# Shift parts given out one at a time in the front, and branch A's sums of group 0 on GpSimd

## The chip, the cores and the metric

The kernel runs on one core of a Trainium2 chip. The time is the device time of one execution in microseconds (us), the median of the runs. Engines are named as in the profile: PE (TensorE matmul), PEld (its weight loads), DVE (VectorE), ACT (ScalarE), POOL (GpSimd), SP (SyncE, which here only issues DMAs). "SPq" is SP's queue. L12 is line 12 of the kernel before.

## The reference

Two attention branches on the same x (1 x 2048 x 512, float32) are mixed by a gate per position:

```
g = sigmoid(sum(x * gate_w))                       # per position
a = A(x):  q, k, v = x @ A_wqkv  (32 heads of 16)
           each position attends to itself and to 7 earlier ones, 2 apart (mask below 0)
           out = softmax(q.k * 16**-0.5) . v, then @ A_wo
b = B(x):  q = x @ B_wq (32 heads of 16), ONE k = x @ B_wk and v = x @ B_wv for all heads
           full softmax over 2048 keys, then @ B_wo
out = g * a + (1 - g) * b
```

## The kernel before

**The stages.** The kernel has a front and a second phase. In the front, PE computes branch B's keys and queries, and then branch A's projections. In the second phase 512 steps compute branch B's softmax: for each unit (one of 32: four blocks of 512 queries by eight head groups) and each of 16 key tiles PE makes scores (L460), ACT takes exponentials (L462), and PE adds up the weighted values (L470). Branch A's local attention runs on POOL meanwhile (`a_load`, `a_scores`, `a_values`), and at four places PE projects the outputs (`out_phase`, L731).

**The maxima.** B's softmax needs each row's maximum before the exponentials: for each unit 64 products of 128 queries by 512 keys must be made on PE and reduced on DVE. They are "fills", put between PE's other work wherever the planner finds room: pairs in bank `pm` (`fill_pair`, L350) and singles in `ps` or `po` (`fill_one`, L361). In most of branch A's projections another form is used, of which one fill stands for four maxima: PE makes half the difference of two products (`fill_diff`, L409), ACT takes its absolute value (L418), PE makes half their sum (`fill_sum`, L409), and DVE adds and reduces (L428).

**The shifts.** When all 64 maxima of a unit are there (`filled`), DVE reduces and transposes them (L340, L342), ACT rounds them (`shift_a`, L434), POOL makes the remainder `ml` (`shift_c`, L440 and L441), and eight DMAs of 2 KB write the pieces into two extra rows of the unit's query tile `qst` (`shift_b`, L449). The scores then come out with the maximum subtracted. While branch A has work left (`pieces`), all eight are issued from SP. Query tiles exist for eight units, so the front can hold the maxima of eight units (512 of the 2048 products) at most.

**Branch A's projections.** They are 64 "lumps": 4 groups of heads (gg) by 16 position tiles (j). Each lump is 24 matmuls on half the rows (L956), the lower rows to one half of a PSUM bank and the upper rows to the other, and the two halves have to be added. Banks `eb[0]` and `eb[1]` alternate. For group 0 a lump is 402 columns wide instead of 384: it also holds B's v and the gate's sum. There the kernel before copies one half to `two` on ACT (L241), and DVE adds the other from PSUM in three additions (L246 to L249, into `stage`, `vst` and `gate`). For groups 1 to 3 (`a_add`) ACT copies both halves, one straight into the stage buffer (L265, L266), and POOL adds (L272). Every second lump one store writes the stage buffer to the scratch tensor `ad` in memory: in group 0 from ACT's queue (L253), in groups 1 to 3 from SP's (L276). There are two stage buffers, so a buffer is used again after four lumps. After the last lump of a group, `whole` makes its heads available to `a_load`; after group 0 it also starts the gate (`gates`, L283 to L291).

**The order.** The schedule is written out by the program itself, with a planner's clock: `clk` holds an assumed time for PE, ACT and DVE, `pool` one for POOL (in ns), and `free` says when a bank is free. All these are constants of the program, not measurements. A task list holds tuples of a due time and a function; `run_tasks`, called after every third matmul step, emits what is due by PE's clock, in the order of the list. `settle(kind, n)` emits all tasks of a kind but the last n at once. `run_pool` gives out branch A's pieces while `pool` is less than 2500 ns ahead of PE's clock. Each engine executes its instructions in the order in which they were emitted, and so does each DMA queue: a DMA that waits for its data holds up the ones behind it. In `stream`, which puts the projections and the fills together, a new pair of differences is emitted when the last fill's sums are out and

```
max(free["m2"], clk["dve"] - 0.7) <= clk["pe"] + 0.1
```

Of the kernel before, what the change touches and what calls it, by code (L numbers as in the profile page):

```python
# [6 lines left out]
F32 = mybir.dt.float32  # L7
F32R = mybir.dt.float32r
AF = mybir.ActivationFunctionType
# [4 lines left out]
P = 128  # L14
# [3 lines left out]
DH = 16  # L18
NJ = S // P
# [7 lines left out]
HALO = (W - 1) * DIL  # L27
# [5 lines left out]
AN = 3 * AC  # L33
GC = P // AC
GN = GC * AN
VN = DH + 2
NB = 8
# [7 lines left out]
T_R, T_LAT, T_EXP, T_RED2, T_RED1, T_W, T_TTR = 0.23, 0.20, 0.92, 1.14, 0.61, 1.21, 0.66  # L45
# [3 lines left out]
def gated_mix_kernel(ctx, tc, xt, wa, wk, wq, wo_a, wo_b, out):  # L49
# [30 lines left out]
    def after(eng, ready, dur):  # L80
        clk[eng] = max(clk[eng], ready) + dur
        return clk[eng]
# [142 lines left out]

    def a_post(gg, j, x):

        (bank, key), n = front[x], GN + (0 if gg else VN)
        for kind in ("post0", "post1", "add") if not gg else ("post0", "post1"):
            settle(kind, 0)  # L230
        if j % 2 == 0:
            settle("store", 1)
            stage["t"] = p1.tile([P, GC, 2, AN], F32, name="stage", bufs=2)
        st = stage["t"]
        if gg:
            return a_add(gg, j, x, st, bank, key)
        if j < 3:
            two = wp.tile([P, GN + VN], F32, name="two", tag="aext", bufs=2)
        else:
            two = pm[0].tile([P, GN + VN], F32, name="two", bufs=1)  # L240
        nc.scalar.activation(two[:, :n], bank[:, 1, :n], AF.Copy)  # L241
        at = after("act", clk["pe"] + T_LAT, 0.45) + 0.1
        free[key] = at + 1.5

        def rest():
            nc.vector.tensor_add(st[:, :, j % 2, :], bank[:, 0, :GN].rearrange("p (g n) -> p g n", g=GC), two[:, :GN].rearrange("p (g n) -> p g n", g=GC))  # L246
            if gg == 0:
                nc.vector.tensor_add(vst[:, j, 0:DH], bank[:, 0, GN:GN + DH], two[:, GN:GN + DH])
                nc.vector.tensor_add(gate[:, 1, j:j + 1], bank[:, 0, GN + DH:GN + DH + 1], two[:, GN + DH:GN + DH + 1])  # L249
            free[key] = after("dve", at, 0.5 if gg else 0.75) + 0.1  # L250
            if j % 2 == 1:
                dst = ad[gg * GC:(gg + 1) * GC, HALO:, :].rearrange("g (p j) n -> p g (j n)", j=NJ)
                tasks.append((free[key], lambda: nc.scalar.dma_start(dst[:, :, (j - 1) * AN:(j + 1) * AN], st.rearrange("p g j n -> p g (j n)")), (), "store"))  # L253
            if j == NJ - 1:
                tasks.append((free[key] + 0.5, whole, (gg,)))

        tasks.append((at, rest, (), f"post{x % 2}"))

    def a_add(gg, j, x, st, bank, key):

        settle("add", 1)
        tag = ("two", "raw", "own")[j % 3]
        two = (p2 if j % 3 else pm)[0].tile([P, GN], F32, name="two", tag=tag, bufs=1)
        own = st[:, :, j % 2, :]
        nc.scalar.activation(own, bank[:, 0, :GN].rearrange("p (g n) -> p g n", g=GC), AF.Copy)  # L265
        nc.scalar.activation(two, bank[:, 1, :GN], AF.Copy)  # L266
        at = after("act", clk["pe"] + T_LAT, 0.8)
        free[key] = at + 0.1

        def rest():  # L270
            nonlocal pool
            nc.gpsimd.tensor_add(own, own, two.rearrange("p (g n) -> p g n", g=GC))  # L272
            pool = max(pool, 1e3 * at) + 1000
            if j % 2 == 1:
                dst = ad[gg * GC:(gg + 1) * GC, HALO:, :].rearrange("g (p j) n -> p g (j n)", j=NJ)
                tasks.append((pool / 1e3 + 0.5, lambda: nc.sync.dma_start(dst[:, :, (j - 1) * AN:(j + 1) * AN], st.rearrange("p g j n -> p g (j n)")), (), "store"))  # L276
            if j == NJ - 1:
                tasks.append((pool / 1e3 + 1.0, whole, (gg,)))

        tasks.append((at, rest, (), "add"))  # L280
# [162 lines left out]
        shift_b(v, ml)  # L443

    def shift_b(v, ml):
        for b in range(2):
            dst = qst[v % NB][64 * b + 62:64 * b + 64].rearrange("x i (t q) -> x i t q", t=4).bitcast(F32)
            for g in range(4):
                (nc.gpsimd if b and not pieces else nc.sync).dma_start(dst[:, :, :, 32 * g:32 * g + 32], ml[32 * g + 16 * b:32 * g + 16 * b + 16, :].bitcast(F32))  # L449
        shifted.add(v)  # L450


    pe, pexp, exped = [], {}, {}
# [228 lines left out]
    def stream(seq, mm, done, pooled):  # L682

        at, told = [0, 0], 0
        ended.clear()
        while min(at) < len(seq):
            single, odd = None, -1
            if pend:
                if free[("m1", "po")[pend[0][4]]] <= clk["pe"] + 0.1 and ready_d[pend[0][4]] <= clk["pe"] + 0.4:
                    single, odd = fill_sum, pend[0][4]  # L690
            elif paired() and not half:
                pass
            elif fillable() and free["m1"] <= clk["pe"] + 0.1:
                single, odd = lambda: fill_one(m1, "m1"), half[0][4] if half else 0
            elif pooled and fillable() and free["po"] <= clk["pe"] + 0.1:
                single, odd = lambda: fill_one(po, "po"), half[0][4] if half else 0
            dur = 0.0
            for b in (0, 1) if odd != 1 else (1, 0):
                if b == odd:
                    now = clk["pe"]  # L700
                    single()
                    clk["pe"] = now
                elif at[b] < len(seq):
                    dur = mm(b, seq[at[b]])
                    at[b] += 1
            after("pe", 0, dur or T_R)
            if ended:
                pass
            elif paired():
                if not half and not pend and max(free["m2"], clk["dve"] - 0.7) <= clk["pe"] + 0.1:  # L710
                    fill_diff()
            elif slots and fillable() and free["m2"] <= clk["pe"] + 0.1:
                clk["pe"] = max(clk["pe"], free["m2"])
                fill_pair(m2, "m2")
            while told < min(at):
                told += 1
                done(seq[told - 1])
# [81 lines left out]
    def settle(kind, n):  # L799
        for task in [t for t in tasks if t[3:] == (kind,)][:-n or None]:  # L800
            tasks.remove(task)
            task[1](*task[2])
# [133 lines left out]
    def mm(b, at):  # L936
        nonlocal pool
        x, i = at
        lump = lumps[x]
        if x not in items:  # L940
            if lump[0] == "a" and lump[1:] == (0, 0):
                settle("rest", 0)
                p0.release()
                branch_a()
                pm.append(tc.alloc_tile_pool(name="maxima", bufs=1, side="right"))
            settle(f"post{x % 2}", 0)
            if lump == ("a", 0, 3):
                half_sel()
            elif lump in (("a", 0, 4), ("a", 0, 6)):
                half_keys(1 if lump[2] == 4 else 0)  # L950
            items[x] = queries(lump[1]) if lump[0] == "q" else a_project(*lump[1:])
            clk["pe"] = max(clk["pe"], free["m2" if x == last else f"e{x % 2}"])
        n = 512 if lump[0] == "q" else GN + (0 if lump[1] else VN)
        l, r = items[x][i]
        h = slice(64 * b, 64 * b + 64)
        nc.tensor.matmul(front[2 if x == last else x % 2][0][:, b, :n], l[h], r[h], start=(i == 0), stop=(i == 3 * C - 1))  # L956
        return T_R if n == 512 else 0.18

    def done_mm(at):
        nonlocal pool  # L960
        x, i = at
        lump = lumps[x]
        if i % 3 == 2:
            run_tasks()
            if p2:
                run_pool()
        if x == last - 1 and i == 3 * C - 2:
            ended.add(1)
        if x == last and i in (2, 7):
            settle(f"post{(i - 1) % 2}", 0)  # L970
            exp_pair(0, int(i == 2))
        if i < 3 * C - 1:
            return
        if lump[0] == "q":
            m = lump[1]
            queries_post(m, eb[x % 2])
            free[f"e{x % 2}"] = clk["act"]
            ahead_wa(0, m - 4)
        else:
            gg, j = lump[1:]  # L980
            a_post(gg, j, 2 if x == last else x % 2)
            if gg + 1 < C:
                ahead_wa(gg + 1, j - 2)
# [8 lines left out]
    stream([(x, i) for x in range(len(lumps)) for i in range(3 * C)], mm, done_mm, True)  # L992
    assert not pend
    formed.clear()
    for kind in ("post0", "post1", "add", "store"):
        settle(kind, 0)
    while [t for t in tasks if len(t) > 3]:
        clk["pe"] += 0.2
# [109 lines left out]
```

## Time and profile before

| what | value |
|---|---|
| time, median of 3 runs | 1537.48 us (1534.87 to 1542.45) |
| profiled execution | 1539.43 us, span 1537.6 us from the first to the last instruction |
| mean granted clock of PE | 0.992 |
| busy share PE / DVE / ACT / POOL | 97% / 81% / 80% / 66% |
| group 0, first L241 to last store's issue | 84.3 to 132.4 us |
| groups 1 to 3, first L265 to last L265 | 134.7 to 293.4 us |
| last maxima (L330) | before 1470 us |

PE's busy time is that of pipelined matmuls, so 97% is not 97% of what PE could do. A share over the span says little here, because the stages have different limits; the prediction goes by the stage that the change touches. "Granted clock" is the share of full speed at which the chip lets PE run.

### The profile page before, as it was taken

How to read it: one execution, taken by the hardware profiler on the slowest of the kernel's cores; microseconds unless marked ns; L12 is line 12 of the kernel's file. 1: busy time of each engine (PE TensorE's matmuls, PEld its weight loads, DVE VectorE, ACT ScalarE, POOL GpSimd, SP SyncE). 2: the span in 40 equal slices, each digit the busy share in tenths (PEclk: the TensorE clock that was granted, in tenths of full speed). 3: DMA queues.
4: the chain of work that ended last, by engine and by line, in shares of the span. 5: the costliest groups of instructions: out<-in, count | busy, mean ns of one | idle time of the engine just before them, and what ended most of it. 6: DMA issues, size and time to landing. Idle time of an engine off the chain costs nothing.

```text
span 1537.6 us, 29033 instructions
## 1 busy us (share of the span) xinstructions
PE 1491.8 (97%) x11020; PEld 717.7 (47%) x11020; DVE 1250.2 (81%) x1794; ACT 1232.9 (80%) x1532; POOL 1016.9 (66%) x1725
## 2 busy tenths in 40 slices
PE   7999988999999999999999999999999999999997
PEld 4989878633333333333333453333453354333532
DVE  6987555688888889888898998888998899888821
ACT  4547766888999999999999759999759966998676
POOL 7833867888978888888988988888886132000320
PEclk9999989999999999999999999999999999999999
DMA  6743223220120211211211112202110000000000
GB/s 214 203 116 130 74 73 94 79 75 22 65 70 16 85 51 43 68 46 40 75 40 41 67 39 68 62 18 68 41 57 22 2 15 16 2 2 1 2 1 28
DMA packets 43908, 85.63 MB, mean 56 GB/s; under 512 B 9520, under 2 KB 25960, under 8 KB 39672
## 3 DMA queue, kind: packets, MB, share of 16 engines
q1 hardware_dynamic: 31976, 40.85, 8.9%
q0 software_dynamic: 6560, 37.95, 7.3%
q10 hardware_dynamic: 5232, 4.98, 1.0%
q8 instruction: 86, 1.41, 0.4%
q14 instruction: 54, 0.44, 0.1%
HBM read 57.97 MB, written 25.25 MB: 54 GB/s over the span
## 4 chain that ended last, share of the span: by engine, by line
PE 85%; DVE 5%; ACT 4%; POOL 2%; SPq 1%; DMA 1%; issue 1%; DVEq 0%; ACTq 0%; POOLq 0%
PE po L470 32%; PE pe L460 22%; PE pm L330 9%; PE ps L330 8%; PE pe L956 5%; PE pe L731 5%; ACT pexp L462 3%; DVE mx L350 3%; DVE mx L361 2%; SPq L449 1%; PE pe L174 1%; PE pm L409 1%; POOL stage L272 1%; DMA ad<-stage 1%; ACT dd L418 1%
## 5 line engine op out<-in xcount | busy, mean ns | idle before, releaser
L462 ACT ACTIVATE pexp<-pe 128x1024 f32<-128x1024 f32 x1024 | 991.7, 1022 | 98.8 <-PE pe L460 95.9
L350 DVE TENSOR_REDUCE mx<-pm 128x2 f32<-128x1024 f32 x563 | 687.1, 1220 | 125.1 <-PE pm L330 120.2
L470 PE MATMUL po<-pexp,vst 128*32 128x512 f32 x4096 | 545.5, 605 | 1.0 <-DVE tt L484 0.5
L460 PE MATMUL pe<-qst,kst 64*128 64x512 f32 x2048 | 464.8, 450 | 9.8 <-ACT pexp L462 4.8
L460 PEld LDWEIGHTS pe<-qst,kst 64*128 64x128 f32 x2048 | 191.3, 183 | 514.1 <-ACT pexp L462 500.5
L361 DVE TENSOR_REDUCE mx<-ps 128x1 f32<-128x512 f32 x568 | 385.8, 679 | 5.5 <-PE ps L330 4.7
L330 PE MATMUL pm<-kst,qst 62*128 62x512 f32 x1139 | 239.7, 408 | 2.3 <-DVE mx L350 1.8
L330 PE MATMUL ps<-kst,qst 62*128 62x512 f32 x568 | 230.6, 406 | 0.8 <-DVE mx L361 0.8
L530 POOL TENSOR_TENSOR pr<-aext 128x256 f32<-128x256 f32 x256 | 182.6, 741 | 2.6 <-DMA aext<-ad 2.4
L590 POOL TENSOR_TENSOR oa<-oa,av 128x256 f32<-128x256 f32 x224 | 164.3, 733 | 15.1
L470 PEld LDWEIGHTS po<-pexp,vst 128*32 128x32 f32 x4096 | 80.5, 108 | 179.4 <-issue 166.4
L587 POOL TENSOR_TENSOR av<-aext,lg 128x256 f32<-128x256 f32 x224 | 139.6, 623 | 13.5
L496 POOL TENSOR_TENSOR rl<-rl,gate_t 128x16 f32<-128x16 f32 x31 | 6.9, 222 | 180.5 <-DVE rl L490 180.3
L330 PEld LDWEIGHTS pm<-kst,qst 62*128 62x128 f32 x1139 | 110.4, 186 | 27.2 <-DVE mx L350 23.1
L330 PEld LDWEIGHTS ps<-kst,qst 62*128 62x128 f32 x568 | 105.7, 186 | 25.6 <-DVE mx L361 20.6
L956 PE MATMUL pe<-wah,xh 64*128 64x384 f32 (+1 forms) x504 | 112.0, 349 | 3.0 <-DVE gate L249 1.7
L956 PE MATMUL pe<-wah,xl 64*128 64x384 f32 (+1 forms) x504 | 112.7, 347 | 0.0
L428 DVE CUSTOM_DVE_ANT_0 dd<-ps,dd 128x512 f32<-128x512 f32 x78 | 53.9, 691 | 71.6 <-PE ps L409 36.9
L956 PE MATMUL pe<-wal,xh 64*128 64x384 f32 (+1 forms) x504 | 111.9, 345 | 0.0
L418 ACT ACTIVATE dd<-pm 128x512 f32<-128x512 f32 x156 | 85.3, 600 | 28.6 <-PE pm L409 26.5
L536 POOL TENSOR_TENSOR tr<-pr 128x512 f32<-128x512 f32 x64 | 81.7, 1277 | 4.3
L536 POOL TENSOR_TENSOR tr<-tr 128x256 f32<-128x256 f32 (+1 forms) x128 | 72.5, 567 | 8.6
(172 smaller groups left out, 1582.4 us busy)
## 6 DMA issues: line engine op xcount, KB each, us to landing
aext<-ad POOLq DMA_DIRECT2D x32, 1056.0 KB, 5.5
ad<-stage SPq DMA_DIRECT2D x24, 384.0 KB
qst<-qd SPq DMA_DIRECT2D x64, 128.0 KB
xraw<-xt SPq DMA_DIRECT2D x16, 256.0 KB
qd<-qhi SPq DMA_DIRECT2D x16, 256.0 KB
qd<-qlo SPq DMA_DIRECT2D x16, 256.0 KB
qst<-qd SPq DMA_DIRECT2D x64, 64.0 KB
qst<-ml SPq DMA_DIRECT2D x228, 2.0 KB
```

The source lines that it names most:

```text
L330: nc.tensor.matmul(dst, qst[v % NB][b:b + 62, pr, t * P:(t + 1) * P], kst[b:b + 62, kc * 512:(kc + 1) * 512], start=True, stop=True)
L350: nc.vector.tensor_reduce(m[:, :, pr, t, kc], dst, AX.X, ALU.max)
L361: nc.vector.tensor_reduce(m[:, odd, pr, t, kc:kc + 1], dst, AX.X, ALU.max)
L418: nc.scalar.activation(dd[0][:, odd], m2[:, odd, :], AF.Abs)
L460: nc.tensor.matmul(bank[:, odd, :], kst[b:b + 64, kt * P:(kt + 1) * P], qst[u % NB][b:b + 64, pr, :], start=True, stop=True)
L462: nc.scalar.activation(e, bank, AF.Exp, scale=SCALE)
L470: nc.tensor.matmul(po[32 * i:32 * i + 32, :], vst[:, kt, :], pexp[s, i // 2][:, i % 2, :], start=(kt == 0), stop=(kt == NJ - 1))
L530: nc.gpsimd.tensor_mul(pr[:, k], q, e[:, o:o + NH, AC:2 * AC])
L536: nc.gpsimd.tensor_add(nx, cur[:, :, 0:n], cur[:, :, n:2 * n])
L587: nc.gpsimd.tensor_mul(av, e[:, o:o + NH, 2 * AC:].rearrange("p j (h d) -> p j h d", d=DH), lg[:, w].unsqueeze(3).to_broadcast([P, NH, AG, ...
L590: nc.gpsimd.tensor_add(ao, ao, av)
L956: nc.tensor.matmul(front[2 if x == last else x % 2][0][:, b, :n], l[h], r[h], start=(i == 0), stop=(i == 3 * C - 1))
```

## The change

Four things change.

- Group 0's sums go the way of groups 1 to 3. ACT now makes four copies per lump (both halves, and one half of v and of the gate's column), and POOL makes the three additions. The PSUM bank is free after ACT's copies. The stores of group 0 are issued from SP's queue. The planner charges ACT 1.2 us and POOL 1.45 us for such a lump, and DVE nothing. The old tasks `post0` and `post1` are gone.
- `settle("add", 1)` holds for all groups, and the buffer `two` rotates over three places in group 0 as well (from j = 3).
- In the front, `shift_b` no longer emits the eight DMAs of a unit together: each is a task of its own, 0.8 us of the planner's clock after the one before. In the second phase they are emitted together as before.
- The condition for a new pair of differences has `clk["dve"] - 1.2` instead of `- 0.7`.

```diff
--- before.py
+++ after.py
@@ -225,52 +225,33 @@
 
     def a_post(gg, j, x):
 
+        nonlocal pool
         (bank, key), n = front[x], GN + (0 if gg else VN)
-        for kind in ("post0", "post1", "add") if not gg else ("post0", "post1"):
-            settle(kind, 0)
+        settle("add", 1)
         if j % 2 == 0:
             settle("store", 1)
             stage["t"] = p1.tile([P, GC, 2, AN], F32, name="stage", bufs=2)
         st = stage["t"]
-        if gg:
-            return a_add(gg, j, x, st, bank, key)
-        if j < 3:
+        if gg == 0 and j < 3:
             two = wp.tile([P, GN + VN], F32, name="two", tag="aext", bufs=2)
         else:
-            two = pm[0].tile([P, GN + VN], F32, name="two", bufs=1)
-        nc.scalar.activation(two[:, :n], bank[:, 1, :n], AF.Copy)
-        at = after("act", clk["pe"] + T_LAT, 0.45) + 0.1
-        free[key] = at + 1.5
-
-        def rest():
-            nc.vector.tensor_add(st[:, :, j % 2, :], bank[:, 0, :GN].rearrange("p (g n) -> p g n", g=GC), two[:, :GN].rearrange("p (g n) -> p g n", g=GC))
-            if gg == 0:
-                nc.vector.tensor_add(vst[:, j, 0:DH], bank[:, 0, GN:GN + DH], two[:, GN:GN + DH])
-                nc.vector.tensor_add(gate[:, 1, j:j + 1], bank[:, 0, GN + DH:GN + DH + 1], two[:, GN + DH:GN + DH + 1])
-            free[key] = after("dve", at, 0.5 if gg else 0.75) + 0.1
-            if j % 2 == 1:
-                dst = ad[gg * GC:(gg + 1) * GC, HALO:, :].rearrange("g (p j) n -> p g (j n)", j=NJ)
-                tasks.append((free[key], lambda: nc.scalar.dma_start(dst[:, :, (j - 1) * AN:(j + 1) * AN], st.rearrange("p g j n -> p g (j n)")), (), "store"))
-            if j == NJ - 1:
-                tasks.append((free[key] + 0.5, whole, (gg,)))
-
-        tasks.append((at, rest, (), f"post{x % 2}"))
-
-    def a_add(gg, j, x, st, bank, key):
-
-        settle("add", 1)
-        tag = ("two", "raw", "own")[j % 3]
-        two = (p2 if j % 3 else pm)[0].tile([P, GN], F32, name="two", tag=tag, bufs=1)
+            two = (p2 if j % 3 else pm)[0].tile([P, GN + VN], F32, name="two", tag=("two", "raw", "own")[j % 3], bufs=1)
         own = st[:, :, j % 2, :]
         nc.scalar.activation(own, bank[:, 0, :GN].rearrange("p (g n) -> p g n", g=GC), AF.Copy)
-        nc.scalar.activation(two, bank[:, 1, :GN], AF.Copy)
-        at = after("act", clk["pe"] + T_LAT, 0.8)
+        nc.scalar.activation(two[:, :n], bank[:, 1, :n], AF.Copy)
+        if gg == 0:
+            nc.scalar.activation(vst[:, j, 0:DH], bank[:, 0, GN:GN + DH], AF.Copy)
+            nc.scalar.activation(gate[:, 1, j:j + 1], bank[:, 0, GN + DH:GN + DH + 1], AF.Copy)
+        at = after("act", clk["pe"] + T_LAT, 0.8 if gg else 1.2)
         free[key] = at + 0.1
 
         def rest():
             nonlocal pool
-            nc.gpsimd.tensor_add(own, own, two.rearrange("p (g n) -> p g n", g=GC))
-            pool = max(pool, 1e3 * at) + 1000
+            nc.gpsimd.tensor_add(own, own, two[:, :GN].rearrange("p (g n) -> p g n", g=GC))
+            if gg == 0:
+                nc.gpsimd.tensor_add(vst[:, j, 0:DH], vst[:, j, 0:DH], two[:, GN:GN + DH])
+                nc.gpsimd.tensor_add(gate[:, 1, j:j + 1], gate[:, 1, j:j + 1], two[:, GN + DH:GN + DH + 1])
+            pool = max(pool, 1e3 * at) + (1000 if gg else 1450)
             if j % 2 == 1:
                 dst = ad[gg * GC:(gg + 1) * GC, HALO:, :].rearrange("g (p j) n -> p g (j n)", j=NJ)
                 tasks.append((pool / 1e3 + 0.5, lambda: nc.sync.dma_start(dst[:, :, (j - 1) * AN:(j + 1) * AN], st.rearrange("p g j n -> p g (j n)")), (), "store"))
@@ -443,11 +424,18 @@
         shift_b(v, ml)
 
     def shift_b(v, ml):
-        for b in range(2):
-            dst = qst[v % NB][64 * b + 62:64 * b + 64].rearrange("x i (t q) -> x i t q", t=4).bitcast(F32)
-            for g in range(4):
-                (nc.gpsimd if b and not pieces else nc.sync).dma_start(dst[:, :, :, 32 * g:32 * g + 32], ml[32 * g + 16 * b:32 * g + 16 * b + 16, :].bitcast(F32))
-        shifted.add(v)
+        for k in range(8):
+            if pe:
+                shift_d(v, ml, k)
+            else:
+                tasks.append((clk["pe"] + 0.8 * k, shift_d, (v, ml, k)))
+
+    def shift_d(v, ml, k):
+        b, g = divmod(k, 4)
+        dst = qst[v % NB][64 * b + 62:64 * b + 64].rearrange("x i (t q) -> x i t q", t=4).bitcast(F32)
+        (nc.gpsimd if b and not pieces else nc.sync).dma_start(dst[:, :, :, 32 * g:32 * g + 32], ml[32 * g + 16 * b:32 * g + 16 * b + 16, :].bitcast(F32))
+        if k == 7:
+            shifted.add(v)
 
 
     pe, pexp, exped = [], {}, {}
@@ -707,7 +695,7 @@
             if ended:
                 pass
             elif paired():
-                if not half and not pend and max(free["m2"], clk["dve"] - 0.7) <= clk["pe"] + 0.1:
+                if not half and not pend and max(free["m2"], clk["dve"] - 1.2) <= clk["pe"] + 0.1:
                     fill_diff()
             elif slots and fillable() and free["m2"] <= clk["pe"] + 0.1:
                 clk["pe"] = max(clk["pe"], free["m2"])
@@ -943,7 +931,6 @@
                 p0.release()
                 branch_a()
                 pm.append(tc.alloc_tile_pool(name="maxima", bufs=1, side="right"))
-            settle(f"post{x % 2}", 0)
             if lump == ("a", 0, 3):
                 half_sel()
             elif lump in (("a", 0, 4), ("a", 0, 6)):
@@ -967,7 +954,6 @@
         if x == last - 1 and i == 3 * C - 2:
             ended.add(1)
         if x == last and i in (2, 7):
-            settle(f"post{(i - 1) % 2}", 0)
             exp_pair(0, int(i == 2))
         if i < 3 * C - 1:
             return
@@ -992,7 +978,7 @@
     stream([(x, i) for x in range(len(lumps)) for i in range(3 * C)], mm, done_mm, True)
     assert not pend
     formed.clear()
-    for kind in ("post0", "post1", "add", "store"):
+    for kind in ("add", "store"):
         settle(kind, 0)
     while [t for t in tasks if len(t) > 3]:
         clk["pe"] += 0.2
```

## The prediction

> **What bounds the kernel now.** I read the page first, then a table of stages, then the waits and the chain in the worst stages.
>
> ```profile
> PE 1491.8 (97%) x11020; PEld 717.7 (47%) x11020; DVE 1250.2 (81%) x1794; ACT 1232.9 (80%) x1532; POOL 1016.9 (66%) x1725
> PEclk9999989999999999999999999999999999999999
> ```
>
> TensorE carries the kernel nearly everywhere; the one dip of the clock is in slices 5 and 6, inside the front. The table by stage (columns: window, length, then busy us of PE, PEld, DVE, ACT and POOL, granted clock, DMA share, GB/s) starts at output group 0 and goes through groups 1 to 3:
>
> ```profile
> 116.00:132.50 16.50, 16.29 (x166) 15.61 (x164) 14.00 (x51) 11.46 (x24) 1.36 (x3) 1.00 0.24 73
> 132.50:172.00 39.50, 36.30 (x355) 33.85 (x353) 23.22 (x73) 31.05 (x74) 28.35 (x37) 0.94 0.42 136
> 172.00:213.00 41.00, 34.05 (x321) 32.56 (x321) 19.47 (x63) 26.46 (x61) 28.65 (x58) 0.85 0.21 63
> 213.00:254.00 41.00, 35.24 (x352) 33.74 (x352) 22.67 (x71) 28.68 (x63) 30.24 (x44) 0.92 0.32 101
> 254.00:296.00 42.00, 39.00 (x397) 35.75 (x393) 25.50 (x79) 34.34 (x70) 35.41 (x54) 1.00 0.26 84
> ```
>
> Group 0, whose sums DVE makes, keeps PE full (16.29 of 16.50). In groups 1 to 3 PE idles 18.9 us and runs part of the time at half clock. The waits from 133 to 297 us say on what:
>
> ```profile
> ACT stage L265 <- DMA ad<-stage: 18.5, 4, 7.0
> PE pm L409 <- ACT dd L418: 15.0, 3, 6.4
> ```
>
> Four times ACT's copy into a stage buffer waits for the store that empties it; PE then waits for ACT. The chain of waits of the longest:
>
> ```profile
> 195.42 0.25 POOL ml L441
> 195.68 0.37 POOL tr L536
> 196.04 0.28 SPq L449
> ...
> 200.31 0.61 SPq L449
> ...
> 200.97 2.70 DMA ad<-stage
> ...
> 205.67 0.79 PE pm L409
> ```
>
> Eight shift parts stand in SP's queue ahead of the store. They wait for ml (195.67), then take eight issues of some 0.65 us, 5.2 us in all; the store lands 2.7 us after its issue. Its sum had been ready since 191.8 (L272 started 190.77 and takes 1.02). The other three have the same form: the parts at 158.16, 238.04 and 276.18, each 5.2 to 5.6 us, then the store.
>
> **The spaced parts.** The eight emissions become tasks 0.8 us of the program's clock apart, and a store that comes due meanwhile is emitted between them. What goes in front of it is then the wait for ml (not changed: part 0 is still emitted at once) and, I estimate, one to three parts, since a store is due 0.5 us after POOL's clock, which may run up to 2.5 us ahead. Five to seven parts at 0.65 are 3.3 to 4.6 us less per store. The PE gaps in the trace are 2.82 (165.28 to 168.10), 6.41 (to 205.67), 5.8 (to 248.08) and 1.1 us (at 285): 16.1 us. The first and the last go wholly; of the second 1.8 to 3.1 us stay, of the third 1.2 to 2.5. Gain: 2.8 + 1.1 + (3.3 to 4.6) + (3.3 to 4.6), so 10.5 to 13.1 us. No other row prices it, so below nothing is bounded by the rival further down.
>
> After three of the gaps PE runs at clock 0.50: 5.9, 4.7 and 4.3 us long, half of it lost, 3.0 + 2.4 + 2.1 = 7.5 us. The 1.1 us gap left the clock at 1.00, the 2.82 us gap did not. So 3.0 us come back surely and 4.5 more if the gaps left stay short: 3.0 to 7.5, I take 5. Together 17 us, ends 13.5 and 20.6. (The Trainium skill, "TensorE: Matmul & The Clock Gate", Part 1, has the clock halve after an idle window of about 3.4 us, which is free-running; by that all 7.5 us would return, but the 2.82 us gap here halved it already, so I stay with the rows.)
>
> **Group 0's additions.** The durations:
>
> ```profile
> L246 DVE TENSOR_TENSOR stage<-pe,two x16: 518/552/558, 86.2 to 131.8; 128x384 f32<-128x384 f32 x16
> L272 POOL TENSOR_TENSOR stage<-stage,two x48: 997/1016/1038, 137.9 to 294.5; 128x384 f32<-128x384 f32 x48
> ```
>
> Removed from DVE per lump: 0.55 + 0.16 + 0.15, 16 times 0.86 = 13.8 us. Added on POOL: 1.02, and two small ones of which the nearest row is L574 (128x16, 0.22): 1.46, 16 times 23.4 us; POOL is busy 8.2 of the 48.5 us from 84 to 132.5, so that hides it, and without that cover it would cost 16 x 0.6 = 9.6 us. Added on ACT per lump: the copy L265, start to start 0.38, and two small copies (nearest rows L291, 32x16, 0.23, and L324, 128x64, 0.35): 0.84 to 1.1 us. Two fill copies cost ACT 0.96 start to start; with 1.4 of them per lump, the old copy's 0.40 and 0.15 of other work, ACT comes to 2.75 to 3.0 us in a lump of 2.93 us: about full. ACT loses the stores (8 issues of 0.37). So 0 to 1.5 us lost over the ten lumps that have such fills. Against it, PE waited 1.7 us for the gate's addition on DVE before it could reuse a bank, and up to 92 us the chain goes through DVE's maxima, two lumps' additions among them (1.7 us): 1.5 to 3.4 us gained. Net gain 0 to 3, I take 1.5.
>
> Queues: the eight stores leave ACT's queue for SP's, behind the shift parts at 89.6 and 121.3. The copies of group 0 now also wait for stage buffers, which the old `two` copies didn't. Branch A's first load waits on POOL for group 0's last store, with the first additions of group 1 behind it; it comes 2 to 3 us later than 137.27. Three summand buffers and the stage buffer not needed before 146.56 hide it; uncovered it costs those 2 to 3 us. The gates' exponential then waits for POOL in place of DVE, and only the gate_t copies follow from it.
>
> **The fill rule, 0.7 to 1.2.** By the program's own clock a pair of differences and its sums now repeats every 1.85 us (DVE's clock 2.52 us after the start, less 0.7 and the 0.1 allowed, at the next 0.18 us step), then every 1.49 (both sums must be out, and m2 free). Groups 1 to 3 hold 261 matmuls of L409, 65 such fills in 48 lumps or 1.36 each; the cycle would allow a quarter more, ACT's copies in it less. I estimate 0.2 to 0.4 more per lump, 10 to 19, and about 3 in group 0: 17. The cap is 512 maxima (eight units); the front holds 422, which leaves 22 fills. In the front a fill costs PE about 0.45 us (0.235 for the pair, 0.1 or so for each sum). Later it saves this much less, a step with three maxima against a step with none:
>
> ```profile
> 605.02 1.00 PE po L470 x8
> 607.15 1.01 PE po L470 x8
> ```
>
> ```profile
> 1475.81 0.99 PE po L470 x8
> 1479.83 0.99 PE po L470 x8
> ```
>
> 2.13 us against 4.02 / 2 = 2.01 (two steps lie between the second pair): 0.04 per maximum, 0.16 per fill of four, for without fills ACT's exponentials set the pace. So each fill moved costs 0.29 us: 17 x 0.29 = 5 us lost, ends 3 and 6.5; nothing is gained except if fills fall into gaps of PE.
>
> **Sum.** The profiled run took 1539.43 us (span 1537.6), 2 us over the median of 1537.48. -17 - 1.5 + 5 = -13.5, ends -20.6 - 3 + 3 = -20.6 and -13.5 + 0 + 6.5 = -7.0: 1525.9 against the profiled run, some 1524 against the median. I give 1525, own range 1517 to 1533.
>
> **Rivals.**
> *The store still comes last (the change does not do what it says).* Part 0 blocks SP until ml is there, and if the store falls due only after 5.6 us of the program's clock, all eight parts precede it as now. For: POOL's clock may be 2.5 us ahead and the tasks run only every third matmul step. Against: in all four cases the sum was ready before or at ml. Half the waits gone and the fills paid: -8 - 1.5 + 5, about 1535; none gone, 1543. Chance 0.22.
>
> *Slower: the wait spreads to group 0.* Group 0's ACT copies now write stage buffers, and their stores share SP with the parts at 89 and 121 us. If a store there lands after its buffer's next use, it is the same stall: 23.6 us over four, 5.9 each. Two in group 0 and one for the unit that 17 more fills complete make 17.7; with 5 for the fills, and half of the old stalls cured (-8 to -12): +11 to +15, near 1552. It decides at the slack of four lumps, 11.7 us, less 4 us for copies and sums, 0.4 and 2.7 for the store: more than 4.6 us behind ml and parts. The stalls in groups 1 to 3 passed this because ml itself came late. Against: at 89.36 and 121.04 ml was ready within 1 us. Chance 0.15.
>
> *GpSimd becomes the bound.* POOL is busy 122.65 of 163.5 us in groups 1 to 3; with the stalls gone it is near 85%, and its in-order additions could hold ACT. From 216 to 238 POOL lies on the chain, yet seven lumps took 20.1 us, 2.87 each, the pace of PE. Should group 0's additions show instead, 9.6 us go: 1535. Chance 0.05. (The Trainium skill, "GPSIMD Engine Reference", 4.1 Engine selection, advises VectorE for elementwise additions, GpSimd being about 2x slower; 1.02 against 0.55 here, 1.85x, agrees, and by that rule this part is a loss.)
>
> **How the numbers follow.** The forecast has 0.58. A measurement can tell about 0.5% (7.7 us): faster is below 1529.8, slower above 1545.2. Of the forecast nearly all, 0.54, is faster, 0.04 the same; of the first rival 0.06 faster, 0.15 the same, 0.01 slower; of the second 0.15 slower; of the third 0.02 faster, 0.03 the same. Faster 0.62, same 0.22, slower 0.16. For 8 in 10 the range goes from 1513 (all 23.6 us back, few fills) to 1546, which leaves out most of the slower case.
>
> **What would show it.** Right: stores L276's line between the L449 issues on SP; L265's wait for the store under 8 us; granted clock over 0.95 in each of the three low windows; the start of the second phase near 275 to 280 us in place of 293; 78 pairs of L418 become about 95. Wrong: L265 or the new copies of group 0 waiting for stores 15 us or more; L956 waiting for ACT before 132 us; POOL additions ending the waits of ACT.

## The result, and the profile after

The changed kernel takes 1521.89 us (median of 4 runs, 1520.65 to 1523.47), the kernel before 1536.69 us over its runs beside them: ratio 0.9896, 95% interval 0.9874 to 0.9918. That is 14.8 us or 1.0% faster. 1525 with a range of 1513 to 1546 had been forecast. The profiled execution took 1523.47 us (span 1521.7), 16.0 us less than the profiled one of before. The line numbers of the changed kernel differ: L240 and L241 are ACT's copies, L250 POOL's addition, L257 the store, L436 the shift parts, L390 and L399 the half differences and ACT's Abs, L458 the weighted values.

From the page of the changed kernel:

```profile
PE 1490.4 (98%) x11020; PEld 708.1 (47%) x11020; DVE 1236.0 (81%) x1748; ACT 1245.8 (82%) x1590; POOL 1035.8 (68%) x1773
PEclk9999999999999999999999999999999999999999
```

14.2 us have gone from DVE; ACT and POOL have 13 and 19 more. The dip of the clock in slices 5 and 6 is gone. The same stages as before (columns: window, length, busy us of PE, PEld, DVE, ACT, POOL, clock, DMA share, GB/s):

```profile
116.00:132.50 16.50, 16.08 (x162) 14.75 (x160) 9.54 (x31) 13.89 (x42) 9.17 (x22) 1.00 0.24 74
132.50:172.00 39.50, 38.91 (x392) 34.97 (x389) 26.28 (x82) 34.54 (x82) 30.61 (x42) 1.00 0.44 136
172.00:213.00 41.00, 40.37 (x406) 36.21 (x406) 27.62 (x87) 35.23 (x81) 35.68 (x67) 1.00 0.30 88
213.00:254.00 41.00, 38.68 (x372) 34.67 (x370) 26.36 (x82) 31.34 (x68) 31.88 (x47) 0.96 0.28 86
```

SP's queue, at one of the shifts:

```profile
192.73 3.91 SPq L436 DMA_DIRECT2D qst<-ml  x6
196.74 0.36 SPq L257 DMA_DIRECT2D ad<-stage  x1
197.15 1.26 SPq L436 DMA_DIRECT2D qst<-ml  x2
```

The store now goes between the parts, as the prediction said, though here after six of them and not after one to three. At the five shifts from 123 us on it goes after one, three, six, seven and six. No ACT copy waits for a store any more. But another wait has grown there. Waits from 133 to 297 us of the changed kernel:

```profile
PEld pm L390 <- ACT dd L399: 13.0, 34, 2.3
PE pm L390 <- ACT dd L399: 1.9, 1, 1.9
```

Before, PEld waited 17.1 us for ACT's dd in six waits and PE 15.0 us in three, mostly in the same three long gaps; now PEld has 34 short waits and PE one. Where the 16 us came from is told by the first and the last weighted matmul, that is by where the second phase begins and ends. Before and after:

```profile
L470 PE MATMUL po<-pexp,vst x4096: 592/605/617, 294.2 to 1525.9; 128*32 128x512 f32 x196
```

```profile
L458 PE MATMUL po<-pexp,vst x4096: 592/604/617, 282.4 to 1509.9; 128*32 128x512 f32 x196
```

The front is 11.8 us shorter, and the second phase 4.2 us. (By the prediction's terms it would have been some 11 and 3 us: -17 - 1.5 + 17 x 0.45 in the front, 17 x 0.16 in the second phase.) A step is counted from 0, from the first of its eight weighted matmuls in the trace to that of the next. Apart from the steps between which the two kernels place an output projection differently, the changed kernel keeps its lead of 10 to 12 us up to step 464 of 512 and then gains 5 us within 16 steps.

### The profile page after: what moved, and what is told of

Same layout as the page of the kernel before. It is cut to its first block, busy times and chain, and to the rows that moved or that the text cites. A ratio compares the mean times of both kernels' runs of the same rounds, so it can differ in the third digit from the quotient of the medians.

```text
span 1521.7 us, 29098 instructions
## 1 busy us (share of the span) xinstructions
PE 1490.4 (98%) x11020; PEld 708.1 (47%) x11020; DVE 1236.0 (81%) x1748; ACT 1245.8 (82%) x1590; POOL 1035.8 (68%) x1773
## 4 chain that ended last, share of the span: by engine, by line
PE 88%; ACT 6%; DVE 4%; issue 1%; DMA 1%; POOL 0%; SPq 0%; DVEq 0%; ACTq 0%; POOLq 0%
PE po L458 31%; PE pe L448 22%; PE pm L311 9%; PE pe L943 9%; PE ps L311 8%; PE pe L719 5%; ACT pexp L450 3%; ACT dd L399 2%; DVE mx L331 2%; PE pm L390 1%; PE pe L174 1%; PE po L390 1%; PE ps L390 1%; DVE mx L342 1%; DMA xraw<-xt 1%
## 5 line engine op out<-in xcount | busy, mean ns | idle before, releaser
L458 PE MATMUL po<-pexp,vst 128*32 128x512 f32 x4096 | 545.5, 605 | 1.2 <-ACT pexp L450 0.6
L342 DVE TENSOR_REDUCE mx<-ps 128x1 f32<-128x512 f32 x553 | 376.1, 680 | 4.9 <-PE ps L311 4.1
L311 PE MATMUL ps<-kst,qst 62*128 62x512 f32 x553 | 224.4, 406 | 0.8 <-DVE mx L342 0.8
L458 PEld LDWEIGHTS po<-pexp,vst 128*32 128x32 f32 x4096 | 80.6, 108 | 178.2 <-issue 164.9
L311 PEld LDWEIGHTS ps<-kst,qst 62*128 62x128 f32 x553 | 102.9, 186 | 25.4 <-DVE mx L342 20.3
L399 ACT ACTIVATE dd<-pm 128x512 f32<-128x512 f32 x166 | 92.2, 610 | 22.5 <-PE pm L390 11.4
L943 PE MATMUL pe<-wah,xl 64*128 64x384 f32 (+1 forms) x504 | 108.9, 341 | 0.0
L409 DVE CUSTOM_DVE_ANT_0 dd<-ps,dd 128x512 f32<-128x512 f32 x83 | 57.4, 692 | 60.5 <-PE ps L390 30.3
L250 POOL TENSOR_TENSOR stage<-stage,two 128x384 f32<-128x384 f32 x64 | 64.9, 1014 | 29.9 <-ACT two L241 15.5
```

What stands on the lines that cost most here:

```text
L311: nc.tensor.matmul(dst, qst[v % NB][b:b + 62, pr, t * P:(t + 1) * P], kst[b:b + 62, kc * 512:(kc + 1) * 512], start=True, stop=True)
L342: nc.vector.tensor_reduce(m[:, odd, pr, t, kc:kc + 1], dst, AX.X, ALU.max)
L399: nc.scalar.activation(dd[0][:, odd], m2[:, odd, :], AF.Abs)
L458: nc.tensor.matmul(po[32 * i:32 * i + 32, :], vst[:, kt, :], pexp[s, i // 2][:, i % 2, :], start=(kt == 0), stop=(kt == NJ - 1))
```

## The experiments

Three parts were changed: S, the spaced parts; G, group 0's sums on GpSimd; R, the fill rule at 1.2. All eight combinations were run; the table has them with the names of the runs. "Front end" and "second phase" are read from the weighted matmul's line, as above, in one profiled execution of each (the one of before took 2.7 us more than its median); "maxima left" are the matmuls of the maxima that the trace has in the second phase. The ratio is to the runs of before beside them.

| kernel | median us | ratio (95% interval) | front end | second phase | maxima left |
|---|---|---|---|---|---|
| before | 1536.7 | | 294.2 | 1231.7 | 1627 |
| S, "spaced_only" | 1519.8 | 0.9881 (0.9866 to 0.9896) | 273.9 | 1232.9 | 1627 |
| G, "group0_only" | 1542.3 | 1.0028 (1.0017 to 1.0040) | 281.9 | 1246.8 | 1647 |
| R, "rule_only" | 1533.3 | 0.9972 (0.9960 to 0.9983) | 297.3 | 1222.7 | 1591 |
| S+G, "after_rule07" | 1530.9 | 0.9960 (0.9948 to 0.9973) | 270.0 | 1247.0 | 1647 |
| S+R, "spaced_rule" | 1526.5 | 0.9928 (0.9910 to 0.9946) | 292.2 | 1222.7 | 1591 |
| G+R, "after_together" | 1524.7 | 0.9918 (0.9901 to 0.9934) | 283.9 | 1227.4 | 1607 |
| S+G+R, the changed kernel | 1521.9 | 0.9896 (0.9874 to 0.9918) | 282.4 | 1227.5 | 1607 |

The first four runs took one part each, and the rule out of the changed kernel.

**The spaced parts alone.**

```diff
 def shift_b(v, ml):
-    (eight DMAs)
+    for k in range(8):
+        if pe: shift_d(v, ml, k)
+        else: tasks.append((clk["pe"] + 0.8 * k, shift_d, (v, ml, k)))
```

> Theory (the stores' stalls are the gain): the kernel before with the spaced parts alone loses most of the 16.1 us of PE gaps and of the 7.5 us of half clock in groups 1 to 3: 1516 to 1525 us against 1536.7, L265's waits for ad<-stage under 8 us, no window at clock under 0.95. Rival (it takes group 0's move or the fill rule as well, which shift the stores against the shifts): 1532 to 1538 us, L265 still waiting 14 us or more.

1519.79 us. The front ends 20.3 us earlier and the second phase is what it was, with the same maxima left. Waits of this kernel from 84 to 280 us:

```profile
ACT stage L265 <- DMA ad<-stage: 2.9, 2, 2.5
```

18.5 us before. So it is shown that the stall was the stores' wait behind the parts, and the size is in the forecast range: 13.5 to 20.6 us had been worked out, 17 taken. The way is another than forecast, though. The store that stood behind all eight parts in the kernel before, at 200.97 us, now goes ahead of them all:

```profile
190.58 0.36 SPq L276 DMA_DIRECT2D ad<-stage  x1
194.44 3.91 SPq L455 DMA_DIRECT2D qst<-ml  x6
```

So does the store that was issued at 243.30 us (now at 224.46, the parts from 227.36 on). These two had 13.3 of the 18.5 us (7.0 and 6.3). Part 0 is now a task as well, is emitted one run of the task list later, and a store that is due by then passes it. Of the other two stores one goes after seven parts, and 2.5 us of its wait of 3.2 stay; one goes after three.

The spaced parts alone are as fast as the whole change: 2.1 us less by the medians, with intervals that overlap.

**Group 0's move alone.**

```diff
-two <- half 1 on ACT; stage, vst, gate <- three additions on DVE; store from ACT's queue
+four copies on ACT; three additions on POOL; store from SP's queue
```

> Group 0's sums on GpSimd alone, parts together and the rule at 0.7. Theory: it gains nothing, since group 0 took the same 50 us in the changed kernel, and it adds waits for stores behind eight parts: 1535 to 1545 us. Rival (DVE relieved is the gain): 1525 to 1531 us, with group 0 some 3 us shorter and the rest the same.

1542.30 us, as the theory said, but not by its reason alone. The stores do stall (waits from 84 to 297 us):

```profile
ACT stage L240 <- DMA ad<-stage: 12.9, 4, 5.2
```

Yet the front is 12.3 us shorter than before, and the second phase 15.1 us longer. It holds 20 maxima more, and the program has a place where they are made up: `pause`, which seven steps before a unit begins stops the steps until enough of its maxima are there. Its chain at step 471 holds:

```profile
1409.38 9.14 DVE mx L331 x8
```

Eight reductions of a pair, one after the other, at 1.14 us each, and PE has nothing else; the granted clock falls with it (window, length, busy PE, PEld, DVE, ACT, POOL, clock, DMA share, GB/s):

```profile
1409.00:1412.00 3.00, 1.22 (x6) 0.56 (x6) 3.00 (x4) 0.00 (x0) 0.00 (x0) 1.00 0.00 0
1412.00:1416.00 4.00, 2.67 (x8) 0.86 (x6) 4.00 (x4) 0.00 (x0) 0.00 (x0) 0.57 0.01 2
1416.00:1420.00 4.00, 1.43 (x6) 1.16 (x7) 2.68 (x4) 0.55 (x1) 0.00 (x0) 0.50 0.02 4
```

Step 471 took 14.5 us in place of 2.1, and step 455 in this kernel 7.6. The kernel before has one such pause, a step of 5.2 us at 471, and the changed kernel none. That is 3.1 of its 5 us between steps 464 and 480; the other 2 us are steps of 1.9 us in place of 2.1, with two maxima in place of three.

**The rule alone.**

```diff
-max(free["m2"], clk["dve"] - 0.7) <= clk["pe"] + 0.1
+max(free["m2"], clk["dve"] - 1.2) <= clk["pe"] + 0.1
```

> The fill rule at 1.2 alone. Theory (the rule puts pairs of differences before ACT has freed their bank, and PE waits: PEld pm <- ACT dd was 13.0 us in 34 waits in the changed kernel): the front is 3 to 11 us longer and the second phase 0 to 5 us shorter: 1534 to 1546 us. Rival (fills moved to the front are worth 0.2 us each and the front takes them free): 1528 to 1533 us.

1533.26 us, between the two: the front is 3.1 us longer, as the theory said, and the second phase 9.0 us shorter, more than it said. With 36 maxima fewer left there is no pause; that is 3.1 of the 9.0 us, and the rest is spread over the phase and was not taken apart.

**The changed kernel with the rule at 0.7 (S+G).**

> The changed kernel with the rule back at 0.7. Theory (the rule costs PE some 11 us in the front and gives back 4): 1512 to 1519 us against 1521.9, PEld pm <- ACT dd down from 13 to some 3 us. Rival (the rule is part of the gain): 1525 to 1530 us. Neither: 1520 to 1524 us.

1530.88 us, 0.9 past the rival's end: the theory fell, and the rival is right that the rule is part of the gain. The rule does cost the front 12.4 us (270.0 against 282.4), and PEld's waits did fall to 3.2 us (133 to 272 us), but the second phase gives back 19.5 and not 4. It repairs what group 0's move had broken: without it the two long pauses are back (14.5 and 7.4 us).

From here the theory was: each fill has a price in the front, and a maximum that is missing has a price in the pauses, far more than the 0.04 us of the prediction. The next four runs tested it and filled in the last two combinations.

**Is it the number of maxima, or group 0's move?** The spaced parts with the front's fills ended early, and nothing else:

```diff
-if not half and not pend and max(...) <= ...:
+if not half and not pend and to_go() > 1650 and max(...) <= ...:
```

> Spaced parts alone, with the front's fills ended 20 maxima early (1648 left for the second phase in place of 1627). Theory (what is missing at the unit boundaries is made in pauses, some 0.75 us for each maximum): front 2 us shorter, second phase 14 us longer, pauses at steps 456 and 472: 1529 to 1534 us. Rival (0.04 us for each maximum as in the prediction): 1517 to 1520 us.

1530.51 us (ratio 0.9954, 0.9940 to 0.9968): the front ends at 268.1 and the second phase takes 1247.3 us with 1647 maxima left, the same as with group 0's move (1246.8) to half a microsecond, and it has the same pauses in the same steps. 20 maxima cost 14.4 us, 0.72 each, nearly all in the pauses (steps 455 and 471 take 7.9 and 14.5 us in place of 2.1 and 5.4), and save 5.8 us in the front, where the theory had 2.

**The rule on top of the spaced parts (S+R).**

> Spaced parts and the rule at 1.2, without group 0's move. Theory (group 0's move costs fills in the front, the rule adds them, and the second phase pays for missing maxima with pauses): front end at 276 to 281 us (spaced parts alone 273.9, the rule adds 3 to 7), second phase 1222 us as with the rule alone (1591 maxima, no pause): 1511 to 1517 us, faster than both. Rival (the rule and group 0's move belong together, since DVE must be relieved first): 1520 to 1526 us.

1526.46 us: the theory fell here as well. The second phase is the 1222.7 us it named, but the front ends at 292.2, not 276 to 281. Nine more fills cost the front 18.3 us. The waits from 133 to 272 us show where; with the spaced parts alone the first line is 3.5 us in 4 waits:

```profile
PEld pm L409 <- ACT dd L418: 15.3, 37, 2.2
PEld ps L409 <- DVE mx L428: 4.3, 5, 2.4
PE pm L409 <- ACT dd L418: 3.8, 5, 1.9
PE ps L409 <- DVE mx L428: 2.8, 3, 2.1
```

The rule lets DVE's planned work end up to 1.3 us after PE's clock, so a new pair of differences is put into PE's queue when ACT or DVE still has its bank, and PE stands there. PEld's waits run beside matmuls and are not lost time as they are; but counted by the starts of PE's matmuls, from 84 us to the front's end, the stretches just before and just after such a pair add up to 55.6 us in place of 37.8. That the rule belongs to DVE's relief, as the rival had it, is borne out in part: on top of S+G, ten more fills cost the front 12.4 us, 1.2 each against 2.0. Where the stores still stall, fills are cheap: 0.3 us each for the rule alone, 0.2 for G+R against G. That they fall into gaps which PE has anyway is likely, but was not shown.

**The eight parts together again in the changed kernel (G+R).**

> The changed kernel with all eight parts emitted together again. Theory (the spacing is the gain, whatever else is changed): the stores stall in the front as before, 12 to 20 us more than the changed kernel in the front and the same second phase of 1227 us: 1533 to 1542 us, L240 waiting for ad<-stage 9 us or more. Rival (group 0's move and the rule shift the stores away from the shifts by themselves): 1521 to 1527 us.

1524.65 us: the rival is right. Taken out of the changed kernel, the spacing is worth 2.8 us, not 17 (1.5 by the fronts; the intervals of the two kernels overlap). In this kernel ACT's copies wait 7.6 us for stores from 84 to 294 us, in three waits of at most 2.8 us, although all eight parts go ahead of the store each time. The store behind them is issued 3.7 to 6.9 us after its sum; in the kernel before it was 4.4, 9.2, 8.2 and 6.2 us. The worst two of before had SP standing at part 0 for ml as well (the sum of the store at 200.97 was ready at 191.8, ml at 195.7). Which store a shift meets depends on where a unit's last maximum falls among the lumps, and both other parts move that. Lumps of some 3.1 us in place of 2.9 also leave more slack. How much each of the two does was not taken apart.

**Parts or the wait for ml?** The kernel before with one part of eight for each unit in the front; the other seven are left out there, so the maxima of these units are not subtracted.

> The kernel before with only one of the eight shift parts issued for each unit in the front (seven are left out there, so the maxima of these units are not subtracted). Theory (the issue time of the parts holds the stores back): like the spaced parts alone, L265's wait for ad<-stage down from 18.5 to under 8 us: 1515 to 1524 us. Rival (SP's wait for ml holds the stores back, not the parts): 1530 to 1538 us, L265 still waiting 12 us or more.

1525.44 us (0.9924, 0.9903 to 0.9945), just past the theory's end, and the wait (133 to 297 us) just under its bound:

```profile
ACT stage L265 <- DMA ad<-stage: 7.5, 2, 5.1
```

So 11.0 of the 18.5 us of waiting came from the time of the parts. The 7.5 that remain are two stores behind the one part that waits for ml, issued 4.3 and 3.6 us after their sums. The second releases its buffer only 6.3 us after its issue at 227.23, where the four of before took 2.7 to 2.9; POOL had issued a load of 1056 KB (`aext`) at 227.17. Spacing the parts does better than leaving seven out, because there these two stores go ahead of part 0.

The last four runs went for the price of a fill and for a better kernel.

**A pair of differences only when its bank is surely free** (S+R, with a margin):

```diff
-max(free["m2"], clk["dve"] - 1.2)
+max(free["m2"] + 0.4, clk["dve"] - 1.2)
```

> Spaced parts and the rule at 1.2, but a pair of differences is emitted only 0.4 us of the program's clock after its bank is free by that clock. Theory (the rule at 1.2 puts the pair before ACT has freed its bank, and PE, which works in order, waits there: with spaced parts and the rule PE and PEld waited 26 us for ACT's dd and DVE's mx on ps and pm, with spaced parts alone 8): these waits fall to some 10 us, the front ends at 276 to 282 us, and the second phase takes 1223 to 1231 us: 1514 to 1520 us. Rival (a fill in the front costs PE its 2 us wherever it stands): 1523 to 1528 us.

1520.91 us (0.9884, 0.9864 to 0.9904), just past the theory's end. PE's and PEld's waits for dd and mx on pm and ps fell from 26 to 1.1 us and the front ends at 267.0, the earliest of all. But fewer fills came in: 1639 maxima left, a step of 11.2 us at 471, second phase 1239.5. Against S+R alone this leaves the price open, since 25.2 us and 12 fills went together, 2.1 us each, as the rival has it. Against "spaced_fewer" it does not: two fills more, and the front ends 1.1 us sooner. So a fill that waits for no bank does not cost 2 us, and the waits are what makes it dear; its price without them was not measured.

**The rule at 0.9 with the spaced parts.**

> Spaced parts and the rule at 0.9, between 0.7 (1519.8) and 1.2 (1526.5). Theory (waits for ACT come in by degrees, the pause of 3 us at step 472 goes with the first few extra maxima): front 274 to 281 us, no pause, 1515 to 1522 us. Rival (a fill more costs 2 us in the front from the first on): 1520 to 1525 us.

1519.47 us (0.9875, 0.9855 to 0.9895). It is in the theory's range, but no faster than the spaced parts alone within the intervals. 1615 maxima left, no pause, second phase 1227.1, front end 278.6, with one stall on a store left (a 4.5 us gap of PE at 231 us). That store is issued at 226.26, 3.0 us after its sum, behind eight parts, and 0.7 us after a load of 1056 KB from POOL (225.60). From 226.0 to 230.5 us the load's queue moved 0.89 MB and SP's queue less than 0.01, and the store's buffer is free only at 233.47, 7.2 us after the issue.

**The planner's charge for a lump of group 0** in S+G:

```diff
-at = after("act", clk["pe"] + T_LAT, 0.8 if gg else 1.2)
+at = after("act", clk["pe"] + T_LAT, 0.8)
```

> The changed kernel with the rule at 0.7 and the planner's charge on ACT for a lump of group 0 at 0.8 in place of 1.2. Theory (the charge, not ACT itself, took fills out of the front, and the second phase paid with pauses): about 1630 maxima left instead of 1647, second phase 1231 to 1235 us, front 270 to 275 us: 1515 to 1522 us against 1530.9. Rival (group 0's copies on ACT cost it): front 280 us or more, 1528 to 1532 us.

1519.26 us (0.9877, 0.9851 to 0.9902) against 1530.88. Only a number of the planner changed. 1623 maxima are left in place of 1647, the second phase takes 1230.2 us in place of 1247.0, the front 275.1 in place of 270.0. So the charge is what makes group 0's move cost time, not ACT's copies. With the smaller charge S+G is as fast as S alone (1519.8): the move then costs nothing, and gains nothing.

**The first part later**, on top of the rule at 0.9:

```diff
-tasks.append((clk["pe"] + 0.8 * k, shift_d, (v, ml, k)))
+tasks.append((clk["pe"] + 2.5 + 0.8 * k, shift_d, (v, ml, k)))
```

> Spaced parts and the rule at 0.9, with the first part 2.5 us of the program's clock after the remainder's emission instead of at once. The order of PE, ACT and DVE is that of spaced_rule09 but for what follows from the shifts. Theory (what is left of the stores' lateness is SP standing at part 0 until ml is there, and parts that still come before a store): L265's wait for ad<-stage falls from 5.2 us to under 2, the 4.5 us gap of PE at 231 us goes or shrinks to 2, front 273 to 277 us, second phase 1227 us as before: 1513 to 1518 us against 1519.5. Rival (what is left is GpSimd's late additions and the landing itself): 1518 to 1521 us, with a wait of 3 us or more.

1512.67 us (0.9852, 0.9835 to 0.9868), just past the theory's end: faster than the kernel before by 1.5% and than the changed one by 0.4% (0.9852 against 0.9896; the intervals do not meet), without group 0's move. Against the run with the rule at 0.9 the intervals overlap, but the traces tell them apart. Its waits from 84 to 280 us:

```profile
ACT stage L265 <- DMA ad<-stage: 0.2, 1, 0.2
```

SP no longer stands at part 0 while a store is ready: the largest lateness of a store is 1.8 us. The front ends at 271.9, 6.7 us sooner, and the second phase takes 1226.8 us with the same 1615 maxima. The store of the last stall is now issued at 223.60, before POOL's load (224.89), and no copy waits for it. So being late at the head of SP's queue was the cause of what was left, and the load made the delay of 3.0 us a wait of 5.2.

## Why the prediction was right, and which steps were not

The sum was right (1525 forecast, 1521.9 measured; -13.5 forecast between the profiled runs, -16.0 measured), and the stall that it was built on is real. But two of its three terms had the wrong sign, and that their errors cancelled is luck. In the prediction's own order the medians give -16.9 for the spaced parts, +11.1 for group 0's move on top of them and -9.0 for the rule on top of both, against -17, -1.5 and +5: one error of +12.6 and one of -14.

- **The spaced parts, -17.** Its size was right alone: some 17 us by the medians, 20.3 in the front. The two kinds of gain are there: PE's gaps of 16.1 us are down to one of 2.1, and the clock of the three low windows is 0.96, 1.00 and 1.00 where it was 0.94, 0.85 and 0.92. Not right was the way: the prediction had part 0 emitted at once as before, one to three parts ahead of each store, the first gap gone, and some of the second and third left. In the run the first gap is the one that stays (2.1 of 2.8 us), and the two long ones are gone wholly, because their stores pass part 0. Of the half clock it read 4.7 us behind the second gap; the trace has 0.50 there for 6.0 us. Wrong was also to count the part as a term that adds to the others: beside them it is worth 2.8 us, because they move the shifts against the stores.
- **Group 0's additions, -1.5.** Their direct costs were hidden: ACT, forecast as about full, was busy 13.89 of 16.50 us (84%), and POOL's slack hid its additions (PE busy 16.08 in the same window, 16.29 before). What failed is the step that the edit has no other effect: the planner's 1.2 us on ACT took 20 maxima out of the front, and that costs about 15 us later. Alone the part is 4 to 5 us slower.
- **The fill rule, +5.** All three numbers of this step were off. The change has 5 more fills than before and not 17, since group 0's charge takes 5 away and the rule adds 10. Where the stores do not stall, a fill in the front costs 1.2 to 2.0 us and not 0.45, since PE stands at a bank that is not free. And a maximum fewer in the second phase saves not 0.04 us: that is what a step shows, but where the last units lack maxima the program pauses, and there 20 of them were worth 14 us. The rule's worth depends on what is missing: -9.0 us on S+G, where the pauses are, +6.7 on S alone, near the forecast +5. The pause at step 471, a step of 5.2 us, was there to be read in the profile of before.
- **The rivals.** All eight parts still ahead of the store, as the first rival had it, is what the trace has at one of the changed kernel's six shifts with a store behind, the one in group 0 at 95.22 us. That the wait spreads to group 0 happened there in small: the store is issued 1.6 us after its sum. PE's gap there, at 91.59, is another wait, for the selection matrix and the bank that DVE has (1.78 us), and no store stall followed. GpSimd did not become the bound: busy 31 of 39.5 and 36 of 41 us, with no ACT wait on its additions over 1.2 us in all.
- **The signs that were named.** Right: the store between the parts, ACT's wait under 8 us, the clock over 0.95. Wrong: the second phase begins at 282.4 and not at 275 to 280, and there are 83 pairs of L399 and not 95. The second said that the third term was wrong while the total was right. The first had not followed from the sum: its front terms, -17 - 1.5 + 17 x 0.45, lead from 294.2 to some 283.

## What to carry to other kernels

A queue that works in order is held up by whatever stands at its head waiting for data: give small transfers to it late and one by one, so that a transfer that frees a buffer can pass. Here, giving out the first of them later still brought 6.7 us in the front. In a schedule written by a planner, an assumed duration is itself a change: a charge of 0.4 us more on ACT cost some 12 us, by way of work left over for a worse place. Before pricing work that moves between stages by its steady rate, look for the place where what is missing is made up, here a pause that no step of the steady state shows.

## What the runs showed of the hardware that was not expected

The clock fell to half after gaps shorter than the 2.82 us of the prediction: after the gap of 1.78 us at 91.59 in the changed kernel, 95 to 100 us ran at 0.71. The gap's length alone does not decide: in the run with all eight parts together in the changed kernel, PE has a gap of 1.78 us at 92.03 too, and 94 to 99 us ran at 1.00.

DVE's small addition `wholek`, whose two inputs lie in SBUF, took 0.178 us in the kernel before and 1.036 us in the changed one:

```profile
L372 DVE TENSOR_TENSOR wholek<-ident x1: 178/178/178, 91.4 to 91.4; 128x32 f32<-128x32 f32 x1
```

```profile
L353 DVE TENSOR_TENSOR wholek<-ident x1: 1036/1036/1036, 90.0 to 90.0; 128x32 f32<-128x32 f32 x1
```

POOL's addition ran beside it, from 89.94 for 1.02 us, and both ended together at about 91.0. The Trainium skill's "GPSIMD Engine Reference" (1. Specifications) says that VectorE and GpSimd share SBUF interfaces and contend where a DVE instruction has two SBUF inputs, which fits. In the nine runs without group 0's move the addition took 0.178 to 0.186 us; in the five with it one DVE instruction is held each time. In G and G+R the addition took 0.990 and 0.996 us beside POOL's. In S+G, and in S+G with the smaller charge, it took 0.18 us, having started within 0.02 us of POOL's addition; there the next DVE instruction, a `sel` with one tensor input, took 0.90 us in place of 0.19 and ended some 0.07 us after POOL's, which took 1.07; that is not the case of two inputs, and why it is held stays open. ACT's two small copies from PSUM (128x16 and 128x1) took 0.19 us each, and start 0.07 apart.
